# Reordering the first head pair of a clustered-attention and gated-FFN kernel

## The chip, the cores and the metric

The kernel runs on one core of one Trainium2 chip. A core has five engines with a queue of instructions each, run in order: PE (matmuls), DVE (vector), ACT (activations and copies), POOL (a second, slower vector engine) and SP, which here only issues DMA. They wait for each other by semaphores. Matrix results land in PSUM, which the kernel uses as eight banks. The metric is device time in microseconds of one launch, lower is better.

## What is computed

For 4 batches, 8 heads, 768 positions and 64 features, each query and each key is assigned to the nearest of its head's 16 centroids; a query attends only to keys of the same cluster. The result, with the 8 heads side by side (512 features per position), goes through a gated FFN of width 1536.

```python
q_assign = np.argmax(np.einsum('bhsd,hcd->bhsc', q_n, c_n), axis=-1)
k_assign = np.argmax(np.einsum('bhsd,hcd->bhsc', k_n, c_n), axis=-1)
mask = q_assign[:, :, :, None] == k_assign[:, :, None, :]
scores = scale * np.matmul(q, k.transpose(0, 1, 3, 2))
scores = np.where(mask, scores, -1000000000.0)
...
attn = attn / (np.sum(attn, axis=-1, keepdims=True) + 1e-09)
return np.matmul(attn, v).astype(np.float32)
...
x = np.ascontiguousarray(attn_out.transpose(0, 2, 1, 3)).reshape(B * S, H * D)
...
gate = 1.0 / (1.0 + np.exp(-(x @ w_gate)))
val = x @ w_val
return (gate * val @ w_out).astype(np.float32)
```

## The kernel before

**The mask as rows of the matmul.** Each q and k value is split into two fp16 halves (`hl`: high in columns 0 to 63, low in 64 to 127) and turned so that features lie on partitions. Rows 64 to 79 of the turned tile are then overwritten by a one-hot code of the cluster: ones for the key's own cluster, and on the query's side -1920 for every other cluster. One matmul thus gives score plus mask. The cluster comes from 36 small matmuls with the split centroids `cm` (`lg`), a maximum over 16 (`mx`) and a comparison (`oh`). On the query's side the comparison gives 0 or 1, and line 290 multiplies it by -1920.

**Steps.** A step is one `sc` matmul (128 keys by 384 queries, line 451), one exponential on ACT (`es`, line 456) and, two steps later, three `av` matmuls (line 468). Batch 0 runs in two passes of 48 steps, 12 for each of 4 head pairs: pass A (steps 0 to 47) takes the first half of the queries, pass B (48 to 95) the second half with the same keys. The other batches follow with 96 steps each, from step 96 on. From step 60 FFN pieces (`g`, `th`, `v`, `hT`, `o`) are spread over the steps.

**What sets the order.** The program is written out in order; `at(i, f)` puts a piece of preparation behind step i. For pair p of pass A, which starts at step U = 12p, the split (line 549) is at U-23, the three turns at U-16 to U-14, the logits at U-13, the one-hot at U-12 and its placement at U-9. Pair 0 is prepared ahead of step 0, pair 1 mostly so. The turn is six PE transposes into a bank (`t_ps`, line 571) and a copy to SBUF (574 on ACT, 576 on DVE). The placement turns the one-hot (`oh_ps`), copies it to `ohT` (607) and moves its four parts to rows 64 to 79 by four small DMAs from SP, here called hops (line 312): key and query rows of head 0, then of head 1. Only pair 0 is placed without DMA, by copies straight from PSUM (599 to 602), which take turns between DVE and ACT.

**Banks.** All preparation, the scores and the gate and value products of the FFN share one ring of four PSUM banks (line 68); two more (`op`, line 70) are for the FFN's result alone and stand empty until its first result, long after step 66. Two hold `av`.

**Loads.** q, k and v of batch 0 are loaded by SP (and one by ACT) at the start. The six weight DMAs (768 KB each in fp16, cast on the way) are issued from POOL's queue at steps 2, 8, 16 and 22, behind whatever POOL has in front of them.

**Start.** POOL clears `warm` for some dummy matmuls; DVE, ACT and PE make `cm`; DVE splits the keys of head 0 and the queries of pair 0, POOL the keys of head 1; DVE copies `identh`, the fp16 identity that every turn needs (line 640).

## Time and profile before

| | us |
|---|---|
| median of 2 runs | 367.94 (367.67 to 368.2) |
| the profiled execution, by its own clock | 367.52 |
| its span, first to last instruction | 365.7 |

The span lacks 1.8 us of the execution's own time. Stages of the span, each named by its first `sc` or `es`:

| stage | from, us | to, us | length, us |
|---|---|---|---|
| start, up to the first exponential | 0 | 19.61 | 19.61 |
| steps 0 to 11 (pair 0) | 19.61 | 29.39 | 9.78 |
| steps 12 to 23 (pair 1) | 29.39 | 38.53 | 9.14 |
| steps 24 to 35 (pair 2) | 38.53 | 47.26 | 8.73 |
| steps 36 to 47 (pair 3) | 47.26 | 55.83 | 8.57 |
| steps 48 to 71 (half of pass B) | 55.83 | 73.82 | 17.99 |
| the rest | 73.82 | 365.7 | 291.9 |

A row of the timeline gives start, length, engine, line and operation, output from inputs, and in brackets how long the engine was idle before it and what ended that. "PEclk" is the clock that was granted to PE, 1.00 being full speed.

### The profile page before, as it was taken

What the parts mean: (1) busy time and instruction counts of PE and PEld (TensorE: products, weight loads), DVE (VectorE), ACT (ScalarE), POOL (GpSimd) and SP (SyncE); (2) the same over time, 40 slices, a digit from 0 to 9 for tenths busy, and PEclk for the clock granted to TensorE, in tenths of its full rate; (3) what the DMA queues carried; (4) which work ended last, traced back from release to release, by engine and by line L of the source; (5) the groups of instructions that cost most, each with busy time, mean ns of one, the idle gap of its engine ahead of it and who ended that gap; (6) DMA issues with size and microseconds to landing.
All of it is one profiled execution on the core that took longest, in us unless ns stands there. A gap on an engine that the chain in (4) does not pass through costs nothing.

```text
span 365.7 us, 8639 instructions
## 1 busy us (share of the span) xinstructions
PE 332.8 (91%) x3267; PEld 205.7 (56%) x3267; DVE 180.9 (49%) x443; ACT 232.9 (64%) x532; POOL 102.1 (28%) x154
## 2 busy tenths in 40 slices
PE   4688679789998989999999998999999999999995
PEld 1566455456555645546666565556665665565552
DVE  5545434777554837645664555527562442242330
ACT  3276558568677868867887687667877786232321
POOL 6756102521234334340424141323301001000000
PEclk9989969999999989999999999999999999999999
DMA  7839965674769686785665778535752110300102
GB/s 263 258 43 212 203 124 188 144 186 81 214 166 197 178 132 163 152 212 132 178 147 128 132 198 154 145 120 44 102 56 68 59 23 0 109 1 31 58 0 87
DMA packets 82138, 46.53 MB, mean 127 GB/s; under 512 B 61040, under 2 KB 79024, under 8 KB 82096
## 3 DMA queue, kind: packets, MB, share of 16 engines
q1 hardware_dynamic: 78000, 41.03, 47.0%
q0 software_dynamic: 3680, 4.72, 7.6%
q8 instruction: 25, 0.41, 0.4%
q10 hardware_dynamic: 416, 0.23, 0.2%
q14 instruction: 17, 0.14, 0.1%
HBM read 28.34 MB, written 6.29 MB: 95 GB/s over the span
## 4 chain that ended last, share of the span: by engine, by line
PE 70%; DMA 16%; DVE 8%; ACT 3%; issue 2%; POOL 1%; SPq 0%; DVEq 0%; POOLq 0%; ACTq 0%
PE o L358 17%; PE v L341 14%; PE g L326 14%; PE sc L451 12%; DMA T<-hl 10%; PE av L468 7%; DMA TA<-ohT 4%; PE lg L263 2%; ACT es L456 2%; DVE t L225 1%; DVE hT L346 1%; PE t_ps L571 1%; DMA cen<-in_centroids_dram 1%; PE oh_ps L308 1%; DVE vs L184 1%
## 5 line engine op out<-in xcount | busy, mean ns | idle before, releaser
L456 ACT ACTIVATE es<-sc 128x384 f16<-128x384 f32 x384 | 172.7, 492 | 56.1 <-PE sc L451 41.6
L468 PEld LDWEIGHTS <-es 128*128 128x128 f16 x1152 | 81.4, 99 | 49.9 <-ACT es L456 8.2
L468 PE MATMUL av<-va,es 128*128 128x65 f16 x1152 | 99.5, 196 | 2.1 <-ACT es L456 0.9
L346 DVE SCALAR_TENSOR_TENSOR hT<-th,v 128x384 f16<-128x384 f32 x96 | 53.0, 552 | 76.0 <-PE av L468 45.2
L451 PE MATMUL sc<-T 80*128 80x384 f16 x288 | 87.6, 329 | 0.3 <-DVE hT L346 0.2
L358 PE MATMUL o<-wo,hT 128*128 128x512 f16 x288 | 70.3, 378 | 0.0
L332 ACT ACTIVATE th<-g 128x384 f32<-128x384 f32 x96 | 47.1, 491 | 28.0 <-DVE hT L346 16.2
L341 PE MATMUL v<-xTb,wv 128*128 128x384 f16 x288 | 58.6, 325 | 0.3 <-DVE hT L346 0.3
L326 PE MATMUL g<-xTb,wg 128*128 128x384 f16 x288 | 58.5, 325 | 0.0
L227 POOL TENSOR_TENSOR xp<-t,rec 128x384 f16<-128x384 f32 x24 | 20.0, 832 | 113.5 <-issue 66.2
L326 PEld LDWEIGHTS <-wg 128*128 128x128 f16 x384 | 37.5, 98 | 24.1 <-issue 3.5
L341 PEld LDWEIGHTS <-wv 128*128 128x128 f16 x384 | 37.3, 97 | 23.5 <-issue 3.4
L358 PEld LDWEIGHTS <-hT 128*128 128x128 f16 x288 | 27.8, 97 | 26.1
L689 POOL TENSOR_TENSOR hl<-kraw,hl 128x384 f16<-128x384 f32 x24 | 22.1, 922 | 47.2 <-DVE hl L688 27.2
L225 DVE TENSOR_TENSOR t<-av,sv 128x390 f32<-128x390 f32 x32 | 18.0, 561 | 20.6 <-PE av L468 20.3
L451 PEld LDWEIGHTS <-T 80*128 80x128 f16 x288 | 27.8, 97 | 0.6
L689 POOL TENSOR_TENSOR hl<-qraw,hl 128x384 f16<-128x384 f32 x24 | 21.9, 912 | 12.9 <-DVE hl L688 12.6
L367 ACT ACTIVATE ob<-o 128x512 f32<-128x512 f32 x16 | 9.6, 597 | 22.4 <-PE o L358 22.3
L277 DVE TENSOR_TENSOR lgs<-lg,lglo 128x192 f32<-128x192 f32 x24 | 8.5, 355 | 27.7 <-ACT lglo L269 27.5
L451 PE MATMUL sc<-TA 128*128 128x384 f16 x48 | 16.9, 377 | 5.1 <-DMA TA<-ohT 4.9
L184 DVE TENSOR_REDUCE vs<-vraw 128x128 f16<-128x768 f32 x12 | 17.7, 1474 | 0.0
L263 PE MATMUL lg<-cm,T 128*128 128x32 f16 x288 | 11.0, 177 | 6.1 <-DMA T<-hl 6.1
(87 smaller groups left out, 278.0 us busy)
## 6 DMA issues: line engine op xcount, KB each, us to landing
kraw<-in_k_dram SPq DMA_DIRECT2D x16, 384.0 KB, 3.9
vraw<-in_v_dram SPq DMA_DIRECT2D x16, 384.0 KB, 4.8
out_dram<-ob SPq DMA_DIRECT2D x24, 256.0 KB, 2.2
qraw<-in_q_dram SPq DMA_DIRECT2D x12, 384.0 KB, 3.9
wg<-in_moe_w_gate_dram POOLq DMA_DIRECT2D x2, 768.0 KB, 10.3
wv<-in_moe_w_val_dram POOLq DMA_DIRECT2D x2, 768.0 KB, 13.7
wo<-in_moe_w_out_dram POOLq DMA_DIRECT2D x2, 768.0 KB, 15.3
qraw<-in_q_dram SPq DMA_DIRECT2D x7, 192.0 KB, 6.5
```

Source lines behind the costliest of these rows:

```text
L184: DVE.tensor_reduce(s[:, :, 0:64], RAW["v", b, p].rearrange("p h c d -> p h d c"), AX.X, ALU.add)
L225: DVE.tensor_tensor(t, av, sv, ALU.add)
L227: eng.tensor_tensor(x, t[..., 0:64], bcast(r, 64), ALU.mult)
L326: PE.matmul(out=g[:, 0:n], lhsT=wg[fc // WQ][:, dc, fc % WQ, :], rhs=xT[:, dc, t0 : t0 + n], start=(dc == 0), stop=(dc == NDC - 1),)
L332: ACT.activation(th[:, 0:n], g[:, 0:n], AF.Tanh, scale=0.5)
L341: PE.matmul(out=w[:, 0:n], lhsT=wv[fc // WQ][:, dc, fc % WQ, :], rhs=xT[:, dc, t0 : t0 + n], start=(dc == 0), stop=(dc == NDC - 1),)
L346: DVE.scalar_tensor_tensor(hT[:, fc, 0:n], st[0][:, 0:n], 1.0, w[:, 0:n], ALU.add, ALU.mult)
L358: PE.matmul(out=o, lhsT=hT[:, fc, bass.ts(t, 128)], rhs=wo[fc // 6][:, fc % 6, :], start=(fc == 0), stop=(fc == NFC - 1),)
L451: PE.matmul(out=sc.rearrange("p (c t) -> p c t", t=128), lhsT=s["k"], rhs=s["q"], start=True, stop=True,)
L456: ACT.activation(es, sc, AF.Exp, scale=SCALE)
L468: PE.matmul(out=av[:, s["c0"] + i, :], lhsT=s["es"][:, bass.ts(i, 128)], rhs=VA[b, p][:, e, s["j"], :], start=(first and i == 0), stop=(la ...
L689: POOL.tensor_tensor(hl[:, :, 64:128], r, hl[:, :, 0:64], ALU.subtract)
```

## The change

It touches only the start, pass A and the preparation of pass B.

1. **The first pair.** DVE clears `warm` and the one-hot tiles; POOL makes `identh` directly. The first k load becomes two DMAs, one for each head. ACT takes the high halves of both key heads, DVE everything else of pair 0's split. The table load for the exponential moves behind `cm`. `first_place` gives way to `first_pair`, which does logits, one-hot and placement head by head: the turned one-hot of head 0 is placed while DVE marks head 1. `v_cast(0, 0)` goes to ACT.
2. **Banks.** Up to step 66 turns, logits, turned one-hots and sums of v use the two `op` banks (`prep_bank`) and not the ring.
3. **The mask factor** -1920 leaves the one-hot (line 290 is skipped in passes A and B) and is applied in the copies: by a per-partition factor `slot_f` in `a_place`, by a constant in `b_place`, by the scale of the copy in `place`.
4. **Pair 1** is turned and marked in steps 0 to 4 and placed in step 6 by four copies from PSUM (`a_place_direct`), without hops.
5. **Tables.** Pairs 2 and 3: split, turns, logits, one-hot and placement at U-25, U-18, U-14, U-13 and U-11 (two steps earlier, logits and one-hot one); the turn that ACT evicted goes to DVE. Pass B: U-22, U-17, U-14, U-13, U-11 (two to three steps earlier).
6. **Weights.** The first two weight DMAs are issued ahead of step 0, the others at steps 6, 14 and 20.

```diff
+    def prep_bank(n=512, dt=FP, name="bank"):
+
+        if step_no[0] > 66:
+            return bank(n, dt, name)
+        return op.tile([128, n], dt, tag="o", name=name)
...
+    make_identity(nc, identh)
...
+    slot_f = const.tile([128, 1], FP, name="slot_f")
+    DVE.memset(slot_f, 1.0)
+    DVE.memset(slot_f[32:64], MASK)
+    DVE.memset(slot_f[96:128], MASK)
...
-    load(SP, "k", 0, 0)
+    for e in range(2):
+        SP.dma_start(out=RAW["k", 0, 0][:, e], in_=view("k", 0, 0)[:, e])
...
         if first:
-            DVE.tensor_copy(hk[:, 0, :, 0:64], k_[:, 0])
+            for e in range(2):
+                ACT.copy(hk[:, e, :, 0:64], k_[:, e])
+            DVE.tensor_copy(hq[..., 0:64], q_)
             DVE.tensor_tensor(hk[:, 0, :, 64:128], k_[:, 0], hk[:, 0, :, 0:64], ALU.subtract)
-            DVE.tensor_copy(hq[..., 0:64], q_)
             DVE.tensor_tensor(hq[..., 64:128], q_, hq[..., 0:64], ALU.subtract)
-            POOL.tensor_copy(hk[:, 1, :, 0:64], k_[:, 1])
-            POOL.tensor_tensor(hk[:, 1, :, 64:128], k_[:, 1], hk[:, 1, :, 0:64], ALU.subtract)
+            DVE.tensor_tensor(hk[:, 1, :, 64:128], k_[:, 1], hk[:, 1, :, 0:64], ALU.subtract)
...
+    def place(t, ps, slot, c0, n, key, eng):
+        src = ps[32 * slot : 32 * slot + 16, 0 : n * 128].rearrange("p (c t) -> p c t", t=128)
+        dst = t[64:80, c0 : c0 + n, :]
+        if eng is ACT:
+            ACT.activation(dst, src, AF.Copy, scale=1.0 if key else MASK)
+        elif key:
+            DVE.tensor_copy(dst, src)
+        else:
+            DVE.tensor_scalar(dst, src, MASK, None, ALU.mult)
+
+    def a_place_direct(p):
+        ps = oh_turn_pe(st0["oh", p], NCH)
+        t = T["A", p]
+        place(t, ps, 0, 0, 6, True, DVE)
+        place(t, ps, 1, 12, 3, False, ACT)
+        place(t, ps, 2, 6, 6, True, DVE)
+        place(t, ps, 3, 15, 3, False, DVE)
...
-        DVE.tensor_copy(ot.rearrange("p c t -> p (c t)"), ps)
+        DVE.tensor_scalar(ot.rearrange("p c t -> p (c t)"), ps, slot_f, None, ALU.mult)
...
+        mx.append(top(lg[0]))
+        mark(lg[0], mx[0], parts(0), mask=False)
+        mx.append(top(lg[1]))
+        for e in range(2):
+            ps = prep_bank(NCH * 128, HP, name="oh_ps")
+            for c in range(NCH):
+                PE.transpose(ps[0:64, bass.ts(c, 128)], oh[:, c, 64 * e : 64 * e + 64], identh)
+            place(t, ps, 0, 6 * e, 6, True, DVE)
+            place(t, ps, 1, 12 + 3 * e, 3, False, ACT)
+            if e == 0:
+                mark(lg[1], mx[1], parts(1), mask=False)
+                dummies(1)
...
-    A_SPLIT, A_TURN, A_LG, A_PICK, A_PLACE, A_V, A_VS = -23, -16, -13, -12, -9, -7, -3
...
+    load_w(0)
+    dummies(2)
+    first_pair()
+
+    for f, s in (
+        (lambda: a_turn(1, [(0, DVE)]), 0),
+        (lambda: v_sum_pe(0, 0), 0),
+        (lambda: turn_pe(T["A", 1], st0["hl", 1], 6, DVE), 1),
+        (lambda: turn_pe(T["A", 1], st0["hl", 1], 12, DVE), 2),
+        (lambda: a_logits(1), 3),
+        (lambda: a_pick(1), 4),
+        (lambda: a_place_direct(1), 6),
+    ):
+        at(s, f)
+    A_SPLIT, A_TURN, A_LG, A_PICK, A_PLACE, A_V, A_VS = -25, -18, -14, -13, -11, -7, -3
...
-        at(U - 20, lambda p=p: b_split(p))
+        at(U - 22, lambda p=p: b_split(p))
...
```

Three places show how this moves instructions. Lines of the changed kernel have its own numbers.

DVE at the start, before: the splits of pair 0 (`hl`), the identity, the centroids, the copies of the turns (`TA<-t_ps`), the one-hot of both heads and the placement.

```order
L555 CAST hl<-kraw 128x6x64
L556 TENSOR_TENSOR hl<-kraw,hl 128x6x64
L557 CAST hl<-qraw 128x6x64
L558 TENSOR_TENSOR hl<-qraw,hl 128x6x64
L640 CAST identh<-ident 128x128
L169 TENSOR_TENSOR cm<-ct_ps,cm 128x8x16
L576 COPY TA<-t_ps 128x768
L562 CAST hl<-qraw 128x6x64
L281 TENSOR_REDUCE mx<-lg_250 128x18
L283 TENSOR_TENSOR oh_173<-lg_250,mx 128x2x6x16
L283 TENSOR_TENSOR oh_173<-lg_250,mx 128x2x3x16
L290 TENSOR_SCALAR oh_173<-oh_173 128x2x3x16
```

DVE at the start, now.

```order
L575 CAST hl<-qraw 128x6x64
L576 TENSOR_TENSOR hl<-kraw,hl 128x6x64
L577 TENSOR_TENSOR hl<-qraw,hl 128x6x64
L578 TENSOR_TENSOR hl<-kraw,hl 128x6x64
L183 TENSOR_TENSOR cm<-ct_ps,cm 128x8x16
L594 COPY TA<-t_ps 128x768 x2
L580 CAST hl<-qraw 128x6x64
L289 TENSOR_REDUCE mx<-lg_264 128x9
L295 TENSOR_TENSOR oh_139<-lg_264,mx 128x6x16
L295 TENSOR_TENSOR oh_139<-lg_264,mx 128x3x16
L289 TENSOR_REDUCE mx<-lg_283 128x9
L619 COPY TA<-oh_ps 16x768
```

The cast of the keys (L555) and that of the identity (L640) are gone from DVE, a subtraction for head 1 (L578) and a second copy of a turn came to it, and the placement of head 0 (L619) now stands ahead of the one-hot of head 1.

POOL around the first weight DMAs, before: the last split of pair 1's keys is long done, L564 to L566 are pair 2's, and `wg_160` to `wv_163` are weights.

```order
L565 TENSOR_TENSOR hl<-kraw,hl 128x6x64
L564 CAST hl<-kraw 128x6x64
L565 TENSOR_TENSOR hl<-kraw,hl 128x6x64
L566 TENSOR_TENSOR hl<-qraw,hl 128x6x64
L135 DMA wg_160<-in_moe_w_gate_dram 128x4x768
L135 DMA wv_161<-in_moe_w_val_dram 128x4x768
L177 MEMSET va 128x12
L178 CAST va<-vraw 128x12x64
L135 DMA wg_162<-in_moe_w_gate_dram 128x4x768
```

POOL around the first weight DMAs, now: L584 is the last piece of pair 1's split, L582 to L584 behind the DMAs are pair 2's.

```order
L584 TENSOR_TENSOR hl<-qraw,hl 128x6x64
L149 DMA wg_175<-in_moe_w_gate_dram 128x4x768
L149 DMA wv_176<-in_moe_w_val_dram 128x4x768
L582 CAST hl<-kraw 128x6x64
L583 TENSOR_TENSOR hl<-kraw,hl 128x6x64
L582 CAST hl<-kraw 128x6x64
L583 TENSOR_TENSOR hl<-kraw,hl 128x6x64
L584 TENSOR_TENSOR hl<-qraw,hl 128x6x64
L191 MEMSET va 128x12
L192 CAST va<-vraw 128x12x64
L149 DMA wg_177<-in_moe_w_gate_dram 128x4x768
```

The first two weight DMAs moved ahead of pair 2's split; the next two still stand behind it and behind the cast of pair 1's v.

DVE around step 62, before, with the semaphores that each row waits for: splits of batch 1 (L688), the FFN's `hT`, and pair 3's split for pass B (L616).

```order
L688 CAST hl<-kraw 128x6x64 [waits Pool_49]
L688 CAST hl<-kraw 128x6x64 [waits DMAHW4_49,Pool_49]
L688 CAST hl<-qraw 128x6x64
L346 SCALAR_TENSOR_TENSOR hT<-th,v 128x384 [waits PE_49,Activation_49]
L633 COPY ohT<-oh_ps 128x384 [waits DMAHW6_49,DMAHW5_49,PE_49]
L616 CAST hl<-qraw 128x6x64 [waits DMAHW0_49,Pool_49]
L346 SCALAR_TENSOR_TENSOR hT<-th,v 128x384 [waits PE_49,Activation_49]
```

DVE around step 62, now: L668 is pair 3's split for pass B, L744 the splits of batch 1.

```order
L685 TENSOR_SCALAR ohT<-oh_ps 128x384 [waits DMAHW3_49,DMAHW2_49,PE_49]
L668 CAST hl<-qraw 128x6x64 [waits Pool_49]
L744 CAST hl<-kraw 128x6x64 [waits Pool_49]
L744 CAST hl<-kraw 128x6x64 [waits DMAHW1_49,PE_49,Pool_49]
L744 CAST hl<-qraw 128x6x64
L365 SCALAR_TENSOR_TENSOR hT<-th,v 128x384 [waits Activation_49] x2
L594 COPY TB<-t_ps 128x768
```

Pair 3's split moved ahead of batch 1's and lost its wait for a DMA; in its place the second L744 got a wait for PE, and the two `hT` and the copy `TB` behind it have none of their own any more.

More of the change, by code (lines that the diff above doesn't have):

```diff
@@ L177, in v_cast @@
         POOL.memset(va[:, :, :, 64:65], 1.0)
-        POOL.tensor_copy(va[:, :, :, 0:64], RAW["v", b, p])
+        (eng.copy if eng is ACT else eng.tensor_copy)(va[:, :, :, 0:64], RAW["v", b, p])
     def v_sum(b, p):
@@ L281, in pick, with mark @@
         DVE.tensor_reduce(mx[:, 0:n], lg, AX.X, ALU.max)
+        return mx
+    def mark(lg, mx, parts, mask=True):
         for a, z, nh, key, o in parts:
@@ L288, in pick @@
             )
-            if not key:
+            if mask and not key:
                 DVE.tensor_scalar(o, o, MASK, None, ALU.mult)
-    ohs = [const.tile([128, NCH, 128], HP, name=f"oh{i}") for i in range(3)]
+    def pick(lg, parts, mask=True):
+        if isinstance(lg, tuple):
+            ls = smp.tile([128, 12, NCL], FP, name="lgs")
+            n = lg[0].shape[1]
+            DVE.tensor_tensor(ls[:, 0:n], lg[0], lg[1], ALU.add)
+            lg = ls[:, 0:n]
+        mark(lg, top(lg), parts, mask)
     oh_n = [0]
@@ L504 @@
     bg = {}
-    step_no = [0]
     def at(i, f):
@@ L638 @@
     centroid_a()
+    cv = centroid_c()
     a_split(0, True)
[L640 to L643 removed]
+    centroid_d(cv)
+    ACT.activation(r0, warm[:, 0:1], AF.Exp)
     dummies(2)
[L645 to L646 removed]
+    a_turn(0, [(0, ACT), (12, DVE), (6, DVE)])
+    v_cast(0, 0, ACT)
     a_split(1)
[L648 to L656 removed]
+    load_w(0)
[12 more added lines that the diff above has]
+    A_SPLIT, A_TURN, A_LG, A_PICK, A_PLACE, A_V, A_VS = -25, -18, -14, -13, -11, -7, -3
     for p in range(1, NP):
```

102 lines of the change are left out of this document (43 added, 59 removed).

## The prediction

> **What bounds the kernel now.** I read the windows of each stage first, then the chain of waits, then where each stage begins, then the prices of single instructions.
>
> ```profile
> 19.00:29.30 10.30, 8.78 (x149) 6.83 (x146) 4.90 (x14) 6.74 (x14) 6.92 (x11) 0.83 0.49 77
> 29.30:38.50 9.20, 7.13 (x117) 5.30 (x118) 5.54 (x16) 5.83 (x13) 4.01 (x6) 1.00 1.16 212
> 38.50:47.20 8.70, 5.49 (x69) 3.64 (x69) 3.20 (x9) 5.02 (x12) 1.72 (x3) 1.00 1.20 204
> 47.20:55.80 8.60, 7.54 (x77) 5.42 (x78) 3.38 (x10) 5.64 (x12) 0.91 (x1) 0.60 0.56 133
> 55.80:61.10 5.30, 5.02 (x69) 3.10 (x70) 3.11 (x10) 4.30 (x11) 0.91 (x1) 1.00 0.34 109
> 61.10:73.80 12.70, 10.81 (x121) 6.98 (x120) 7.97 (x20) 7.92 (x19) 6.38 (x7) 1.00 0.71 174
> 250.00:310.00 60.00, 59.74 (x578) 37.21 (x575) 26.35 (x61) 45.18 (x105) 10.35 (x17) 1.00 0.28 50
> ```
>
> Columns: length, then busy time of PE, weight load, DVE, ACT and POOL, granted clock, DMA share, GB/s. In pass A (rows 1 to 4) no engine is full, and twelve steps take 8.6 to 10.3 us; the first twelve of pass B, with the same work per step, take 5.3. Late in the span PE is busy 59.74 of 60 us: there nothing of this change can help or be regained, so what the start gains is the total gain.
>
> ```profile
> 9.48 0.86 DVE identh L640
> 10.39 2.10 PE t_ps L571 x18
> ...
> 13.35 0.96 PE lg L254 x36
> ...
> 32.84 5.55 DMA TA<-ohT
> ...
> 41.71 5.42 DMA TA<-ohT
> ```
>
> PE's first turns wait for DVE's splits and for the identity (0.86), and later each pair waits for its own hop (the second of four, head 0's query rows), 5.4 to 5.6 us from issue to landing. The stages begin with these rows, of ACT and PE:
>
> ```profile
> 19.61 0.50 ACT L456 ACTIVATE es<-sc 128x384 f16<-128x384 f32 x1
> 29.39 0.32 PE L451 MATMUL sc<-TA 128*128 128x384 f16 x1 [0.93 <-DMA TA<-ohT]
> 38.53 0.32 PE L451 MATMUL sc<-TA 128*128 128x384 f16 x1 [1.27 <-DMA TA<-ohT]
> 47.26 0.32 PE L451 MATMUL sc<-TA 128*128 128x384 f16 x1 [2.65 <-DMA TA<-ohT]
> ```
>
> Pass B begins where the fourth window ends, at 55.8.
>
> **Term a, the start: first exponential at 15.2 instead of 19.61, -4.4.** Prices of one instruction, and the landing of pair 0's queries:
>
> ```profile
> 5.40 2.43 DVE L555 CAST hl<-kraw 128x384 f16<-128x384 f32 x1
> 6.20 2.30 POOL L646 MEMSET oh<- 128x768 f16 x3
> 7.86 0.56 DVE L556 TENSOR_TENSOR hl<-kraw,hl 128x384 f16<-128x384 f32 x1
> 8.46 0.61 POOL L564 CAST hl<-kraw 128x384 f16<-128x384 f32 x1
> 8.75 0.73 DVE L558 TENSOR_TENSOR hl<-qraw,hl 128x384 f16<-128x384 f32 x1
> L562 DVE CAST hl<-qraw 128x384 f16<-128x384 f32 x2 | 0.7, 352 | 0.0
> L574 ACT COPY TA<-t_ps 128x768 f16<-128x768 f16 x4 | 3.2, 798 | 5.9 <-PE t_ps L571 5.9
> L576 DVE COPY TA<-t_ps 128x768 f16<-128x768 f16 x5 | 2.8, 555 | 4.1 <-PE t_ps L571 4.0
> L283 DVE TENSOR_TENSOR oh<-lg,mx 128x192 f16<-128x192 f32 x3 | 1.1, 358 | 0.2
> L599 DVE COPY TA<-oh_ps 16x768 f16<-16x768 f16 x1 | 0.5, 548 | 0.7 <-PE oh_ps L308 0.7
> L600 ACT COPY TA<-oh_ps 16x384 f16<-16x384 f16 x1 | 0.5, 468 | 4.0 <-DVE TA L599 4.0
> L158 ACT ACT_TABLE_LOAD x1 | 1.3, 1283 | 0.0
> 1.19 0.45 ACTq L106 DMA_DIRECT2D qraw<-in_q_dram  x1
> qraw<-in_q_dram ACTq DMA_DIRECT2D x1, 192.0 KB, 4.4
> ```
>
> The queries land at 1.19+4.4 = 5.6, just as DVE is done with the centroids (L555 follows them at 5.40). DVE then does a cast (0.35) and three subtractions (0.56 to 0.73, taken as 0.65): 7.9. ACT's two casts of the keys have no row; bounded by 0.47 (L600) and 0.80 (L574) each, they lie beside that. ACT has the table load (1.28) between the centroids' copy, near 6.2, and its copy of the first turn (0.80), which so ends near 8.4. With two banks the third turn waits for that copy: six transposes at 2.10/18 are 0.7, DVE's copy 0.55, to 9.6. Logits of both heads (0.96) behind two dummies: 11.1. Head 0's one-hot, bounded by the two L283-like pieces at 0.36 each, runs beside head 1's logits: 11.4. Three dummies hold PE until about 12.1; six transposes 0.6, DVE's copy 0.55, head 1's comparison 0.5, six transposes 0.6, DVE's copy 0.55 and ACT's 0.47 give 15.3. The first exponential is queued behind that last copy on ACT; I take 15.2. With PE's share at full clock it is 14.2, with dummies at half clock and subtractions held 16.6: -5.4 to -3.0. The memsets that moved to DVE (2.30 by POOL's row) and the identity are done before the centroids land and cost nothing; without that cover they would add those 2.3. The cast of v on ACT (0.80) lies in ACT's idle time before the placements, else +0.8. One more load on SP moves the later ones by an issue of 0.45; nothing waits for them then.
>
> L555 took 2.43 us beside POOL's memsets; the same cast takes 0.35 (L562). [...]
>
> **Term b, steps 0 to 11: 10.3 instead of 9.78, +0.5.** Pair 1's preparation now lies in these steps, on DVE: five placements and copies before and at step 6, three more turns, in all some sixteen copies, casts and comparisons at 0.3 to 0.56, 7.7; plus PE parts that DVE waits for with two banks (logits twice, one turned one-hot, one sum, 2.6) and nine hand-overs of about 0.1: 11.2, of which 1.1 lie before the first exponential. Ends: 9.3 without hand-overs, 12.5 with PE at half speed. Step 12 needs no hop any more; its placement by copies, about 2.2, is over before. The mask product leaves DVE; where a copy takes it over I take the copy at its old price, 0.55.
>
> **Term c, steps 12 to 23: 9.3 instead of 9.14, +0.2.** The placement moves two steps up, but on DVE it still stands behind the normalisation of the pair before, which ends at the same place in the steps; so the hop is issued no earlier against step 12. The weights are in flight, hence the hop takes 5.4 again. Step 24 at 15.2+10.3+9.3 = 34.8.
>
> **Term d, steps 24 to 35: 7.3 instead of 8.73, -1.4.** DMA work by stretch, and an undisturbed hop:
>
> ```profile
> 3.00:16.00 13.00, 7.65 (x67) 4.16 (x65) 8.73 (x18) 3.55 (x6) 9.80 (x15) 1.00 1.06 353
> ...
> 24.50:49.50 25.00, 18.64 (x298) 13.63 (x294) 12.09 (x31) 15.65 (x36) 10.36 (x17) 0.98 1.15 199
> 23.07 0.94 POOL L135 DMA_DIRECT2D wg<-in_moe_w_gate_dram  x1
> TB<-ohT SPq DMA_DIRECT2D x8, 12.0 KB, 1.7
> ```
>
> Loads fill the DMA engines until 16, and from 24.5 on the weights fill them for 25.0 us. POOL reaches the first weight DMA near 11, so its data starts 1.4 later, near 12.4, while 3.6 us of loads remain: all weights are in at 12.4+3.6+25.0 = 41 instead of 49.5. Pair 3's hop is issued 3.2 after step 24 (41.71 less 38.53), at 38.0, 3 us before the weights' end. It takes between 1.7 and 5.4; I take 4, two thirds of the way, because the weights are still moving: step 36 at 42.1.
>
> **Term e, steps 36 to 47: 6.5 instead of 8.57, -2.1.**
>
> ```profile
> 17.55:20.97 3.42, 2.25 (x51) 1.73 (x48) 2.27 (x5) 2.13 (x5) 0.00 (x0) 1.00 0.00 0
> 20.97:24.38 3.41, 2.97 (x24) 2.06 (x24) 1.59 (x6) 2.24 (x6) 2.16 (x3) 0.50 0.00 0
> 44.86:48.28 3.42, 1.02 (x23) 0.83 (x24) 0.01 (x1) 0.85 (x3) 0.00 (x0) 1.00 1.25 213
> 48.28:51.69 3.41, 2.63 (x23) 1.79 (x23) 2.68 (x9) 1.82 (x5) 0.00 (x1) 0.50 0.46 77
> ```
>
> After the 2.65 us hole the granted clock is 0.50 from 48.28 on and 0.60 in the stage's mean, and there the one-hot for pass B stood behind the normalisation on DVE; it now comes a step earlier. At full clock the stage would take 5.3 as steps 48 to 59 do, at half clock about 8; the longer hole now is the one at step 24, so most of the half clock falls into steps 24 to 35, where the hop sets the end anyway. I take 6.5, nearer the 5.3 row. [...]
>
> **Term f, steps 48 to 71: -0.8.**
>
> ```profile
> DVE hl L616 <- DMA T<-hl: 2.3, 1, 2.3
> PE t_ps L571 <- POOL hl L617: 0.9, 1, 0.9
> ```
>
> Pair 3's split for pass B waited 2.3 for a transposing DMA, and PE 0.9 for it; that goes. Late next is the split of batch 1 (second L744), which on DVE waits for PE's turn of step 67, with two `hT` behind it; PE has scores and gate products to run meanwhile, so I expect no more than 0.5 from it. Ends: +2 (DVE held for the whole 2.3) and -1.9, the 12.70 less 10.81 us in which PE was idle.
>
> **Sum.** -4.4+0.5+0.2-1.4-2.1-0.8 = -8.0. From the profiled execution's 367.52 that is 359.5; the median of the two runs lies 0.42 above it, so 359.9, told as 360.0.
>
> **Rivals.** (1) The hops keep the lead: the third hop costs 5.4 as well, and PE stays at half clock after it. Then d is 0 (3.2+5.4 is the old 8.7 again), e is -0.6, the sum -5.1 and the time 362.8. For it speaks that all three hops cost nearly the same. [...] (3) The hops cost under 3 us, as those of pass B do, and no stage waits for one: steps 12 to 23 and 24 to 35 then take about 7.0 each (9.14 and 8.73 with holes of 1.27 and 2.65 taken off, and a little for the freed ring), c is -2.1 and d -1.7, in sum 357.3; against it all three hops beside the weights. (4) Slower: with two banks, preparation and steps wait for each other in all three first pairs. A pair has about ten turns, sums and logits for which PE must have a bank back from DVE; at 30 of them it decides from 8.0/30 = 0.27 us each over what I counted, and at 0.4 the time is 372. No quoted row shows a hold of that size, but the ring had four banks.
>
> **Chances.** My forecast (358 to 361.5) 0.50, rival 1 0.24, rival 2 0.08, rival 3 0.14, rival 4 0.04. Two per cent, about what a measurement of this kernel can tell from no change, is 7.36 us, so the line is at 360.6. Faster: 0.35 of the forecast's 0.50, rival 3 and a sliver, 0.50; slower 0.02; the same 0.48. The range runs from 356 (rival 3 with 1.3 us less) to 364.5 (rival 1 with 1.7 us more).
>
> **What would show it.** First exponential near 15.2; no hop before step 12; hops of step 24 near 5.4 and of step 36 shorter; weights landed near 41; first score of pass B near 48.6, step 72's near 66. Wrong if DVE's casts at the start again take over 2 us, if PE waits over 1 us for a bank in steps 0 to 11, or if PE waits at step 68 for `hT`.

## The result and the profile after

| | before | after |
|---|---|---|
| median, us | 367.94 (2 runs) | 354.05 (353.22 to 354.87, 2 runs) |
| ratio | | 0.962, 95% interval 0.952 to 0.972 |
| profiled execution: its own time, span | 367.52, 365.7 | 353.22, 351.4 |

The changed kernel is faster by 13.9 us, where 8 were predicted, and 354.05 lies under the predicted range of 356 to 364.5. Run again six times it gave a median of 355.98 (352.62 to 358.11), ratio 0.962 (0.957 to 0.967). All eight executions have a mean of 355.4; two of them, 358.04 and 358.11, count as slow, because they lie over 1.5% above the fastest, and the other six have a mean of 354.4.

The windows of the stages after, with the columns of before (length, busy time of PE, weight load, DVE, ACT and POOL, granted clock, DMA share, GB/s); the first four are steps 0 to 47 in twelves, the fifth steps 48 to 71:

```profile
13.80:24.00 10.20, 7.91 (x162) 6.69 (x162) 6.77 (x16) 5.66 (x13) 7.52 (x12) 1.00 1.15 236
24.00:32.50 8.50, 6.65 (x121) 5.21 (x119) 6.24 (x16) 5.80 (x13) 3.34 (x5) 1.00 1.18 211
32.50:40.20 7.70, 6.41 (x82) 4.76 (x82) 3.83 (x10) 5.36 (x12) 1.72 (x3) 0.78 0.99 170
40.20:46.70 6.50, 5.57 (x78) 3.52 (x79) 3.19 (x9) 5.02 (x12) 0.91 (x1) 1.00 0.22 63
46.70:63.00 16.30, 15.12 (x186) 10.04 (x186) 10.06 (x27) 12.33 (x29) 7.26 (x8) 1.00 0.58 172
```

The rows of the timeline with which stages begin (first exponential, first scores of steps 24 and 36); step 12 now waits for no DMA:

```profile
13.83 0.49 ACT L475 ACTIVATE es<-sc 128x384 f16<-128x384 f32 x1
...
32.52 0.32 PE L470 MATMUL sc<-TA 128*128 128x384 f16 x1 [1.49 <-DMA TA<-ohT]
...
40.19 0.32 PE L470 MATMUL sc<-TA 128*128 128x384 f16 x1 [1.27 <-DMA TA<-ohT]
```

| stage | before, us | after, us | difference | predicted |
|---|---|---|---|---|
| start (a) | 19.61 | 13.83 | -5.8 | -4.4 |
| steps 0 to 11 (b) | 9.78 | 10.15 | +0.4 | +0.5 |
| 12 to 23 (c) | 9.14 | 8.54 | -0.6 | +0.2 |
| 24 to 35 (d) | 8.73 | 7.67 | -1.1 | -1.4 |
| 36 to 47 (e) | 8.57 | 6.52 | -2.1 | -2.1 |
| 48 to 71 (f) | 17.99 | 16.29 | -1.7 | -0.8 |
| the rest | 291.9 | 288.4 | -3.5 | 0 |

The prediction's sum falls short in four places: the start, steps 12 to 23, pass B and, most of all, the rest. Of the rest's 3.5 us, 2.9 lie in batch 1 (steps 96 to 191), where the change moves no instruction. The windows of that batch, before and after:

```profile
96.12:158.13 62.01, 54.51 (x610) 34.29 (x609) 36.34 (x94) 48.36 (x118) 23.93 (x35) 0.97 0.78 179
```

```profile
84.50:143.64 59.14, 52.98 (x610) 33.55 (x609) 36.38 (x95) 47.77 (x118) 23.93 (x35) 1.00 0.76 192
```

PE runs the same 610 matmuls in 62.01 and in 59.14 us. Before, it stood idle for 7.5 us there (62.01 less 54.51), and its clock was not full: one window with PE busy 1.73 of 3.41 is followed by one at half clock, here called a half-clock spell. Of the 2.9 us, 1.5 are busy time (54.51 against 52.98) and 1.3 idle time (7.5 against 6.2).

```profile
130.19:133.60 3.41, 1.73 (x27) 1.14 (x25) 0.55 (x1) 1.79 (x5) 0.90 (x2) 1.00 1.15 155
133.60:137.01 3.41, 3.41 (x33) 2.06 (x30) 1.33 (x5) 2.27 (x5) 0.00 (x0) 0.50 0.51 99
```

The list of waits names the largest part of the idle time: PE's logits wait for the transposing DMA that turns the split halves (`T<-hl`). The two rows, before and then after, are of the whole span (us in total, times, longest); in batch 1 alone the waits sum to 4.8 and 3.3.

```profile
PE lg L263 <- DMA T<-hl: 6.1, 7, 1.7
```

```profile
PE lg L277 <- DMA T<-hl: 4.5, 4, 1.4
```

### The profile page after: what moved, and what is told of

It is laid out like the page before. It is cut to its first block, busy times and chain, and to the rows that moved or that the text cites. A ratio compares the mean times of both kernels' runs of the same rounds, so it can differ in the third digit from the quotient of the medians.

```text
span 351.4 us, 8653 instructions
## 1 busy us (share of the span) xinstructions
PE 326.8 (93%) x3274; PEld 202.2 (58%) x3274; DVE 181.0 (51%) x449; ACT 231.3 (66%) x532; POOL 97.8 (28%) x149
## 4 chain that ended last, share of the span: by engine, by line
PE 72%; DMA 5%; DVE 3%; ACT 3%; issue 2%; POOL 1%; SPq 0%; ACTq 0%; DVEq 0%
PE o L377 18%; PE v L360 16%; PE g L345 15%; PE sc L470 12%; PE av L487 7%; DMA T<-hl 5%; ACT es L475 3%; PE lg L277 2%; DVE hT L365 1%; DVE vs L198 1%; DVE hl L744 1%; DVE t L239 0%; POOL hl L745 0%; PE vs_ps L204 0%; DVE oh L295 0%
## 5 line engine op out<-in xcount | busy, mean ns | idle before, releaser
L487 PEld LDWEIGHTS <-es 128*128 128x128 f16 x1152 | 80.2, 98 | 48.9 <-ACT es L475 8.3
L487 PE MATMUL av<-va,es 128*128 128x65 f16 x1152 | 97.9, 194 | 2.7 <-ACT es L475 1.1
L470 PE MATMUL sc<-T 80*128 80x384 f16 x288 | 86.7, 327 | 0.3 <-DVE hT L365 0.2
L470 PE MATMUL sc<-TA 128*128 128x384 f16 x48 | 15.6, 348 | 2.8 <-DMA TA<-ohT 2.8
L384 DVE TENSOR_SCALAR ob<-o 128x512 f32<-128x512 f32 x8 | 5.5, 690 | 21.0 <-PE o L377 21.0
```

Of the source, the lines that this page charges most:

```text
L470: PE.matmul(out=sc.rearrange("p (c t) -> p c t", t=128), lhsT=s["k"], rhs=s["q"], start=True, stop=True,)
L487: PE.matmul(out=av[:, s["c0"] + i, :], lhsT=s["es"][:, bass.ts(i, 128)], rhs=VA[b, p][:, e, s["j"], :], start=(first and i == 0), stop=(la ...
```

## The experiments

Stage lengths below are taken between the first DVE instruction of the normalisations (`t<-av`), which stand two steps behind each head pair's last score. They are steadier than the time: behind step 36 the two traces of the changed kernel agree within 0.1 us up to batch 1.

| us | first exponential | 0-11 | 12-23 | 24-35 | 36-47 | 48-59 | 60-71 | 72-83 |
|---|---|---|---|---|---|---|---|---|
| before | 19.61 | 10.48 | 9.14 | 9.04 | 7.76 | 7.99 | 12.95 | 9.85 |
| after | 13.83 | 11.28 | 8.11 | 7.68 | 6.01 | 7.50 | 11.99 | 8.79 |
| after, again | 14.53 | 10.72 | 8.35 | 7.23 | 6.01 | 7.50 | 11.98 | 8.80 |
| old start | 18.94 | 10.74 | 9.67 | 6.31 | 6.01 | 7.50 | 11.99 | 8.79 |
| old weight issue | 14.43 | 10.66 | 8.96 | 8.05 | 6.01 | 7.50 | 11.98 | 8.80 |
| ring of four | 13.88 | 9.79 | 8.40 | 7.82 | 6.01 | 7.45 | 12.22 | 8.79 |
| old table, pass B | 15.01 | 12.22 | 11.15 | 7.11 | 6.07 | 7.63 | 12.50 | 9.84 |
| old table, pairs 2, 3 | 15.78 | 11.48 | 8.12 | 7.80 | 6.01 | 7.49 | 11.99 | 8.80 |
| pair 1 by hops | 14.51 | 11.14 | 7.94 | 7.81 | 6.01 | 7.50 | 11.99 | 8.79 |
| old mask factor | 14.72 | 11.09 | 8.90 | 6.26 | 6.01 | 7.50 | 11.99 | 8.79 |

**The changed kernel once more.**

> The changed kernel once more, unaltered, as the base of the runs that undo a part. Theory 'stages' (the gain is 5.8 us of start, 3.3 us of steps 12 to 47 and the rest in stages behind step 48, all set by the order of the program): 354.0 within 0.5, first exponential near 13.8, the same two waits for hops at steps 24 and 36. Theory 'clock' (a good part of the gain is half-clock spells of 3.4 us that were escaped by chance of where the 3.4 us windows lie: four in the trace before, one in the trace after): the number of half-clock spells in the new trace is not one, and each spell more costs up to 1.7 us, so 354.0 to 356.

Six executions spread over 5.5 us. The trace of the fastest, 352.62, is like the first: waits of 1.73 and 0.81 for hops, one half-clock spell at the same place. The spread does not follow the clock alone (358.04 at a mean clock of 0.994, 358.11 at 0.976), so neither theory holds it all; the first fits the traces.

**Undoing the start.**

> The changed kernel with the start of before: one k load, clears of the dummies' input and of the one-hot tiles on POOL, identity copied on DVE, the old split, turns with two copies on ACT, logits, one-hot and placement of both heads together, v cast on POOL. Pair 1 is still turned in steps 0 to 2. Theory 'start adds in full': first exponential near 18.8 (19.61 less the 0.8 of pair 1's turn that stood ahead of it), so 5.0 later and 359.0. Theory 'start is absorbed by the hops': the weights land at the same 38.7, so the hops of pairs 2 and 3, now issued later, meet fewer bytes; 2 us or more of the 5.0 come back by step 48 and the time is 357 or less. With a further half-clock spell at step 0 up to 1.7 more.

```diff
+    DVE.tensor_copy(identh, ident)
...
+    a_turn(0, [(0, ACT), (12, DVE), (6, ACT)])
...
-    v_cast(0, 0, ACT)
...
-    first_pair()
+    a_logits(0)
...
+    a_pick(0)
+    v_cast(0, 0)
+    first_place()
...
```

359.37 us, ratio 0.975 (0.971 to 0.979); first exponential at 18.94. By step 48 the kernel is 4.8 us behind: the start adds in full. It also shows what a hop costs once the weights are in. The landing times of pair 2's four hops, and of pair 3's, issued from 41.3 on (the DMA share is 1.26 in the microsecond from 40 and 0.17 in that from 42):

```profile
L327 SPq DMA_DIRECT2D TA<-ohT x4: 567/707/807, 31.7 to 34.2; - x4
...
DMA to landing us min/median/max: 5.5/5.9/6.7
...
L327 SPq DMA_DIRECT2D TA<-ohT x4: 507/540/580, 41.3 to 43.2; - x4
...
DMA to landing us min/median/max: 1.7/1.8/2.0
```

Same shapes, same sizes: 5.9 us beside the weights, 1.8 behind them, and no wait at step 36.

**Undoing the weight issue.**

> The changed kernel with the weight DMAs issued at steps 2, 8, 16 and 22 again. Theory 'weights set the hops' (the term d of the prediction): first weights move from 10.8 to about 16, the last land near 43 instead of 38.7; the hop of pair 3 then costs its 5.4 and the wait at step 36 grows from 1.27 to about 3: 355.5 to 357. Theory 'hops cost the same' (the queue's own latency and not the weights): waits at steps 24 and 36 stay within 0.3 of 1.49 and 1.27 and the time is 354.0.

```diff
-    load_w(0)
...
+    at(2, lambda: load_w(0))
+    at(8, lambda: load_w(1))
+    at(16, lambda: load_wo(0))
+    at(22, lambda: load_wo(1))
```

356.10, ratio 0.965 (0.961 to 0.969). The weights end some 4 us later (the DMA share falls under 1 in the microsecond from 42 instead of from 38), the waits for hops are 2.10 and 1.56, and the kernel is 1.2 us behind by step 48. The direction is the first theory's, but the wait at step 36, which by it grows to about 3, grew to 1.56 only; the time alone does not tell.

**Undoing the banks.**

> The changed kernel with all preparation in the ring of four banks again, the two result banks empty up to the FFN's first result. Theory 'banks free the steps': scores wait for a ring bank behind preparation that DVE holds, in steps 0 to 11 and in steps 48 to 83, where PE's idle time went from 3.2 to 1.9 us; the time rises by 1 to 2.5, to 355 to 356.5. Theory 'banks do nothing': 354.0 within 0.5. Theory 'two banks hold back' (the fourth rival): PE no longer waits 0.79, 1.05 and 1.62 for copies by DVE and ACT in the start and in steps 0 to 11, and the time falls to 352 or 353.

```diff
     def prep_bank(n=512, dt=FP, name="bank"):
-        if step_no[0] > 66:
-            return bank(n, dt, name)
-        return op.tile([128, n], dt, tag="o", name=name)
+        return bank(n, dt, name)
```

354.42, ratio 0.959 (0.955 to 0.963). Steps 0 to 11 are shorter by 0.9 to 1.5 and pass B is as long as with the two banks (60 to 71 0.2 longer). The two banks give next to nothing and hold the steps beside pair 1 back: the third theory, as far as the trace goes.

**Undoing the table of pass B.**

> The changed kernel with the old table for pass B (split, turn, logits, one-hot and placement two to three steps later). Read by stage lengths between the normalisations of head pairs, which agree within 0.1 us between the two traces of the changed kernel behind step 36 (steps 36 to 47 6.01, 48 to 59 7.50, 60 to 71 11.99, 72 to 83 8.79). Theory 'the table of pass B': the lengths go back towards the 7.99, 12.95 and 9.85 of before, 2.0 to 2.5 us in sum, and steps 36 to 47 gain 0.5 to 1; the mean of the runs (355.4 in eight runs of the changed kernel) rises to 358. Theory 'batch 1 comes in earlier' (loads, splits and the FFN meet the steps otherwise because the start is shorter, whatever the table): the lengths stay within 0.3.

```diff
-        at(U - 22, lambda p=p: b_split(p))
+        at(U - 20, lambda p=p: b_split(p))
...
```

357.75, ratio 0.978 (0.969 to 0.986). Steps 48 to 83 take 1.7 us more, 1.05 of it in steps 72 to 83, where the old length of before is back to 0.01. Steps 36 to 47 do not change. PE's list of waits shows both what the table does and what it doesn't:

```profile
PE sc L470 <- DMA TA<-ohT: 4.1, 1, 4.1
...
PE t_ps L589 <- POOL hl L669: 1.4, 1, 1.4
```

The second row is the table: PE waits for pair 3's split on POOL, as it did before (0.9). The first, a 4.1 us wait at step 24, is not: the program up to step 25 is the same as in the changed kernel, but two half-clock spells fell into the start and steps 0 to 11 of this execution, and its hops took up to 7.2. So the profiled execution's 359.21 overstates the table; the 1.7 us of steps 48 to 83 are its measure.

**Undoing the table of pairs 2 and 3; pair 1 by hops; the mask factor.**

> The changed kernel with the old table for pairs 2 and 3 of pass A (two steps later, logits and one-hot one) and the second turn on ACT. The prediction's step c says that the hop is issued no earlier against its step, because the copy stands behind the normalisation on DVE: by it the waits at steps 24 and 36 stay near 1.5 and 1.0 and the time does not change. Theory 'two steps earlier are two steps less to wait': each hop is issued about 1.2 us later against its step, both waits grow by that, steps 12 to 35 take 2 to 2.5 us more, and more half-clock spells follow the longer holes.

```diff
-    A_SPLIT, A_TURN, A_LG, A_PICK, A_PLACE, A_V, A_VS = -25, -18, -14, -13, -11, -7, -3
+    A_SPLIT, A_TURN, A_LG, A_PICK, A_PLACE, A_V, A_VS = -23, -16, -13, -12, -9, -7, -3
...
```

355.72, ratio 0.973 (0.964 to 0.982). Steps 12 to 35 take 15.92 us, against 15.79 and 15.58: the table does nothing, as step c had it. The hop is issued 2.2 us behind the normalisation here (29.46 less 27.26) and 2.1 behind it in the changed kernel (27.16 less 25.11).

> The changed kernel with pair 1 placed by hops (at step 6, turned and marked in steps 0 to 4 as now). Theory 'the hop of pair 1 sets step 12': issued about 1.3 us behind the one-hot at 17.9, near 19.5, and 4.7 to 5.4 on the way, its second part lands near 25, step 12 waits about 1 for it instead of 0 at 23.98; three copies of 0.56 leave DVE, so steps 0 to 11 take 0.5 to 1.5 us more. Theory 'the copies cost as much as the hop' (DVE is the bound of steps 0 to 11): no change within 0.3, since 1.6 us of copies go.

```diff
...
-        (lambda: a_place_direct(1), 6),
+        (lambda: a_place(1), 6),
...
```

354.15, ratio 0.969 (0.960 to 0.979). Step 12 waits 2.21 for the hop, and steps 0 to 11 are as long as in the changed kernel (11.14 against 11.28 and 10.72): the copies cost about what the hop cost. The edit also puts the sum of v (`v_sum_pe`) ahead of pair 1's first turn.

> The changed kernel with the factor -1920 applied to the one-hot on DVE again (0.56 for head pairs of pass A, 0.20 for pass B) and plain copies. Theory 'it stands in the chain': first exponential 0.2 to 0.5 later, hops of pairs 2 and 3 later by 0.3 to 0.5 each, 1 us in all. Theory 'the factor in the copy costs the copy what it saves': no stage changes by more than 0.3.

```diff
-        DVE.tensor_scalar(ot.rearrange("p c t -> p (c t)"), ps, slot_f, None, ALU.mult)
+        DVE.tensor_copy(ot.rearrange("p c t -> p (c t)"), ps)
...
```

358.55 (353.31 to 358.90), ratio 0.972 (0.955 to 0.989), too wide to tell; in the trace step 48 is reached within 0.1 us of the changed kernel (46.98 against 46.91 and 46.84), so no cost shows.

**Where batch 1 gains: a wait, or the place of the buffers.** First the logits of batches 1 to 3 two steps later, in both kernels.

> The kernel before with the logits and the one-hot of batches 1 to 3 two steps later (and their turned one-hot and hops with them); nothing else. It tests the 2.9 us that the change gained in batch 1 (steps 96 to 191: 62.0 us before, 59.1 after), where it moved no instruction. Theory 'one wait, one spell': before, PE's five waits for transposing DMAs (4.8 us) make one 3.4 us window with PE busy only 1.73, and the next runs at half clock; without the waits the spell near 133 goes too, steps 96 to 191 take 57 to 58.5 and the time falls by 3.5 to 5, to 363 to 364. Theory 'the waits hide other waits' (PE would wait for the exponentials or DVE then): steps 96 to 191 stay above 60.5 and the time within 1.5 of 367.5.

```diff
-            at(s + gap + 9, lambda e=e: lgt(e))
+            at(s + gap + 11, lambda e=e: lgt(e))
...
```

366.29, ratio 0.998 (0.994 to 1.002): nothing. (Its trace is that of the longest of ten executions, 370.12, and is not read by stages.)

> The changed kernel with the same shift of batches 1 to 3. Theory 'one wait, one spell': PE's waits for transposing DMAs there are 3.3 us in the first trace of the changed kernel and 2.7 in the second, without a spell; most of them go, steps 96 to 191 take 57 to 58 instead of 59.1, and the mean of the runs falls from 355.4 to 353.5. Theory 'the waits hide other waits': within 0.5 of 59.1.

353.84, ratio 0.962 (0.957 to 0.967): PE's wait for `T<-hl` in batch 1 falls from 3.3 to 2.3, but its wait for DVE's sums of v grows from 0.9 to 3.0, and batch 1 takes 60.1 instead of 59.1. Here the waits hid other waits, as the second theory has it.

What the change did to those DMAs is in no line that moves an instruction. Its new tile `slot_f` has 4 bytes per partition and takes 32, so the buffers behind it start 32 bytes further on (first tile of each, bytes in a partition, in the built program):

```
              hl               T
before        98528 (32 mod 64, 224 mod 256)    112352 (32 mod 64, 224 mod 256)
after         98560 ( 0 mod 64,   0 mod 256)    112384 ( 0 mod 64,   0 mod 256)
```

> The kernel before with one more tile of 4 bytes per partition (it takes 32) behind the matrix of ones, and nothing else. In the changed kernel the new tile for the mask's factors moves every later SBUF buffer by 32 bytes: the split halves and their turned tiles start at 32 modulo 64 before and at 0 after. The fastest transposing DMA from the one to the other took 3.7 us in both traces of the old layout and 3.2 in all eleven of the new one. Theory 'layout': 3.2 here too, the one of the attention's output slower in turn (2.6 before, 3.2 to 3.5 after), PE's waits for the transposing DMAs in batch 1 fall from 4.8 to about 3, steps 96 to 191 from 62.0 to 59 to 60.5, and the time by 1.5 to 3, to 365 to 366.5. Theory 'neighbours' (the 0.5 comes from what else is in flight or from the order of the queues): 3.7 and 367.5.

```diff
     POOL.memset(ones, 1.0)
+    pad = const.tile([128, 1], FP, name="pad")
+    POOL.memset(pad, 0.0)
```

365.07, ratio 0.988 (0.984 to 0.993), 3.7 us under before in the same session (368.76). Batch 1 takes 57.95, without a half-clock spell, and PE's waits for `T<-hl` in it sum to 1.9. Of the output's two transposing DMAs the small one, whose median the expectation gave, was not slowed (`xB<-xp`, at the fastest 2.3, before 2.4); the larger one was (`xTb<-xp`, 2.7, before 2.5; rows below).

> The changed kernel with the same tile added, which moves the buffers to 32 modulo 64 again. Theory 'layout': fastest transposing DMA of the split halves 3.7, PE's waits for them in batch 1 from 3 to 4.5, steps 96 to 191 60.5 to 62 instead of 59.1, with a half-clock spell in some runs; mean of the runs 357 to 358 instead of 355.4. Theory 'neighbours': 3.2 and the stages unchanged within 0.3.

The same two lines in the changed kernel: 358.82, ratio 0.973 (0.970 to 0.976), 3.4 above the mean of 355.4 and 4.4 above that of 354.4; batch 1 takes 64.45, with two half-clock spells. Now one side of the DMA at a time.

> The changed kernel with the seven turned tiles T alone moved to 32 modulo 64 (32 bytes ahead of them and 32 behind, so that all other buffers keep their place modulo 64). Theory 'target': the fastest transposing DMA of the split halves takes 3.7 here and PE's waits in batch 1 grow to 4 or more; the mean of the runs 357 to 359. Theory 'source': 3.2 and 355.4.

> The changed kernel with the three split tiles hl alone moved to 32 modulo 64, all others kept. Theory 'target': 3.2 and 355.4. Theory 'source': 3.7, and the mean of the runs 357 to 359. If both kernels show 3.7, either side is enough; if both show 3.2 the two must coincide.

```diff
+    pad1 = pool("pad1", 1)
     hlp = pool("hl", 3)
+    pad2 = pool("pad2", 1)
     tp = pool("T", 7)
...
```

(For the target the pads stand around `tp`.) 354.28, ratio 0.963 (0.957 to 0.968), with the target moved; 357.97, ratio 0.975 (0.966 to 0.983), with the source moved. Batch 1 takes 61.22 and 62.67, each time with one half-clock spell, and PE's waits for `T<-hl` in it sum to 3.7 and 5.3. What answers for the split halves in each trace (issues, landing time): before, changed, before with a pad, changed with a pad, target moved, source moved.

```profile
L247 SPq DMA_TRANSPOSE T<-hl x24: 1425/1460/3326, 66.8 to 263.7; - x24
...
DMA to landing us min/median/max: 3.7/3.7/6.9
```

```profile
L261 SPq DMA_TRANSPOSE T<-hl x24: 1301/1422/3422, 58.5 to 248.7; - x24
...
DMA to landing us min/median/max: 3.2/3.3/7.7
```

```profile
L249 SPq DMA_TRANSPOSE T<-hl x24: 1393/1432/3586, 65.1 to 257.7; - x24
...
DMA to landing us min/median/max: 3.2/3.2/7.1
```

```profile
L263 SPq DMA_TRANSPOSE T<-hl x24: 1301/1447/3405, 58.9 to 254.6; - x24
...
DMA to landing us min/median/max: 3.7/3.8/7.5
```

```profile
L265 SPq DMA_TRANSPOSE T<-hl x24: 1301/1423/3514, 58.1 to 250.5; - x24
...
DMA to landing us min/median/max: 3.2/3.3/7.2
```

```profile
L265 SPq DMA_TRANSPOSE T<-hl x24: 1302/1450/3274, 59.1 to 252.5; - x24
...
DMA to landing us min/median/max: 3.7/3.8/7.0
```

Read the minimum and median: 3.2 to 3.3 where the source starts at 0 modulo 64, 3.7 to 3.8 where it starts at 32, whatever the target. The source sets it. For this DMA all starts tried at 0 modulo 64 are also at 0 modulo 256.

Two other transposing DMAs, both of 128x768, tell 64 and 256 apart, because the pads moved their sources along (starts in the built programs): that of the output from batch 1 on (`xTb<-xp`) and that of the one-hot (`ohT<-oh`). First the output's, before (source at 0 modulo 256) and in the kernel `x4_align` below (source at 64):

```profile
L479 SPq DMA_TRANSPOSE xTb<-xp x12: 1211/1228/1590, 115.1 to 310.8; - x12
...
DMA to landing us min/median/max: 2.5/2.8/4.0
```

```profile
L498 SPq DMA_TRANSPOSE xTb<-xp x12: 1210/1240/2205, 101.4 to 293.0; - x12
...
DMA to landing us min/median/max: 2.7/2.9/4.1
```

Then the one-hot's, before with a pad (source at 0 modulo 256, target at 224) and changed with a pad (source at 192, target at 0):

```profile
L704 SPq DMA_TRANSPOSE ohT<-oh x12: 1212/1227/2189, 80.2 to 266.5; - x12
...
DMA to landing us min/median/max: 2.5/3.4/5.5
```

```profile
L760 SPq DMA_TRANSPOSE ohT<-oh x12: 1212/1230/2597, 71.9 to 263.0; - x12
...
DMA to landing us min/median/max: 2.7/2.8/5.6
```

Here the fastest landing is read, since the median also holds waits behind other transfers. In all nineteen traces it is 2.5 where the source starts at 0 modulo 256 (`xTb<-xp` in two traces, `ohT<-oh` in one) and 2.7 elsewhere. Starts at 64 and 192, multiples of 64 too, landed later. Of the starts run (0, 32, 64, 96, 160, 192 and 224 modulo 256) 0 alone landed sooner; 128 was in no run.

Side and size are thus measured: 3.7 for sources at 224 (before) and at 32 modulo 256 (source moved), 3.2 at 0; 2.7 for sources at 64 and 192, 2.5 at 0. Why a start elsewhere lands later is not shown.

**A faster version.**

> The changed kernel with all preparation in the ring of four banks and pairs 2 and 3 placed by four copies as pair 1 is, eight steps ahead, so that pass A has no hop at all. It leaves the weights as they are. Theory 'the hop behind the weights sets steps 24 and 36' (hops took 3.4 to 7.2 us while weights were in flight and 1.7 to 2.0 behind them): both waits and the half-clock spell at 33 go; steps 12 to 23 fall from 8.1 to 6.7, steps 24 to 35 from 7.7 to 6.3; with 1.0 from the ring in steps 0 to 11 the time is 350 to 351.5. Theory 'DVE is the bound of pass A anyway' (pair 1 cost the same by hops and by copies): the copies, 2.2 us a pair less 0.56, take the place of the waits; 353.5 to 354.5.

```diff
-            at(U + A_PLACE, lambda p=p: a_place(p))
+            at(U - 8, lambda p=p: a_place_direct(p))
...
```

350.47, ratio 0.953 (0.947 to 0.960): the first theory. Pass A has no hop and its trace no half-clock spell before 118.

> Both of the two edits above in one kernel. If they add, the time is 1.5 us under that of the direct placement alone: 348.5 to 350 by the first theories of each, 352 to 353.5 by the second ones.

348.86 (348.66 to 349.59), ratio 0.949 (0.943 to 0.955), the fastest and steadiest: the trace has full clock from end to end. Its windows of steps 0 to 47:

```profile
13.10:22.90 9.80, 8.70 (x165) 6.87 (x164) 7.14 (x19) 6.49 (x15) 8.10 (x12) 1.00 1.15 253
22.90:30.70 7.80, 6.76 (x118) 5.18 (x117) 6.01 (x15) 5.59 (x14) 3.35 (x5) 1.00 1.16 209
30.70:37.40 6.70, 5.61 (x86) 3.95 (x84) 4.81 (x14) 5.64 (x15) 1.72 (x3) 1.00 1.24 208
37.40:43.40 6.00, 4.93 (x72) 3.13 (x70) 3.19 (x9) 4.64 (x12) 0.91 (x1) 1.00 0.49 116
```

The weights still fill the DMA engines (share 1.16 and 1.24), but nothing in steps 12 to 35 waits for a small DMA behind them.

> The fastest kernel so far (ring of four banks, direct placement of pairs 2 and 3, logits of batches 1 to 3 two steps later; 348.9) with a tile of 32 bytes ahead of the attention's output, so that the tiles of both transposing DMAs start at 0 modulo 64. Theory 'layout': the transposing DMA of the output falls from 3.2 to 2.6 in the first pass and the split halves stay at 3.2; its waits are few, so the time falls by 0 to 1, to 348 to 349. Theory 'neighbours': no change of either.

349.71, ratio 0.948 (0.944 to 0.951): no further gain. The tile put the output's source at 64 modulo 256 and not at 0, where by the rows above nothing is won: `xTb<-xp` stays at 2.7 at the fastest, and `xB<-xp` has a median of 2.9 instead of 2.8. What fails is the expectation's 64; the output's source at 0 was not run in this kernel.

## Why the prediction was right and wrong

**The rest: wrong, and the largest miss.** The sentence "there nothing of this change can help or be regained, so what the start gains is the total gain" failed twice. It was read from a window at 250 to 310; between step 72 and the end of batch 1 PE was not full (7.5 us idle in batch 1 alone). And it took the change for a change of order only. Shown: the 32 bytes of `slot_f` are worth 3.7 us in the kernel before and 3.4 to 4.4 in the changed one, through the source of the transposing DMA (moved alone 357.97, against 354.28 with the target moved). With a second pad, that is with the change but without this effect, the kernel takes 358.82, inside the forecast's 358 to 361.5.

How 0.5 us per DMA becomes that is shown in part. In the three traces read by stages with the source off a multiple of 256 (before, changed with a pad, source moved), PE's waits for `T<-hl` in batch 1 sum to 4.8 to 5.8 and the batch takes 62.0 to 64.5; in the fifteen with the source on one the waits are 1.7 to 4.0 and the batch takes 58.0 to 61.2. All three have one or two half-clock spells in that batch, of the fifteen only four have one. That the longer waits bring the spells on is argued and not shown.

**Term f: right mechanism, too small.** Predicted -0.8 in steps 48 to 71. The table of pass B is worth 1.7 by the undoing, 1.05 of it in steps 72 to 83, which the term left out. Of the shortening of steps 48 to 71 that leaves 0.8 (7.99 and 12.95 to 7.63 and 12.50) which no undone part brings back; its cause stays open. Pair 3's split is on time, and the turn of batch 1 behind it cost nothing: PE has no wait over 0.25 us for `hT` near step 68.

**Term a: right mechanism, 1.4 us too small.** Part of the first trace's surplus is chance: the centroids landed 0.65 earlier than before (first used at 3.06 instead of 3.71), and ACT's copy of the first turn, which stands behind them and the table load, ends at 7.95 instead of the sum's 8.4. In the second trace of the same kernel they were used at 3.52 and the first exponential came at 14.53; over the fifteen traces with this order of the start it came between 13.10 and 15.78. A further 0.6 is a dummy pair that the sum put on the path. It runs beside DVE's last copy, and the logits, of which only head 1's need that copy, start before it ends (rows of the timeline after). Some 0.3 is left unassigned.

```profile
3.06 0.23 DVE L169 TENSOR_TENSOR sq<-cen 128x64 f32<-128x64 f32 x1 [0.37 <-DMA cen<-in_centroids_dram]
...
7.17 0.78 ACT L592 COPY TA<-t_ps 128x768 f16<-128x768 f16 x1
...
8.33 0.59 PE L562 MATMUL wm<-warm 128*128 128x512 f16 x2
...
8.54 0.56 DVE L594 COPY TA<-t_ps 128x768 f16<-128x768 f16 x1 [0.99 <-PE t_ps L589]
...
8.77 1.05 PE L268 MATMUL lg<-cm,TA 128*128 128x16 f16 x36
```

The slow end of this term's range (16.6) has subtractions that are held. No run shows such a hold. Before, DVE's L558 took 0.73 beside a POOL cast (8.46 to 9.07), 0.17 more than L556. In the changed kernel all three subtractions took 0.55, but it was hardly put to the test there: POOL's first cast began at 6.34, when only the third of them (6.30 to 6.85) was still running. That cast took 0.88 where the next took 0.51, so here POOL was the slower one, not DVE:

```profile
6.30 0.55 DVE L578 TENSOR_TENSOR hl<-kraw,hl 128x384 f16<-128x384 f32 x1
```

```profile
6.34 0.88 POOL L582 CAST hl<-kraw 128x384 f16<-128x384 f32 x1 [4.29 <-DMA kraw<-in_k_dram]
```

**Term b: right in size.** 10.15 against 10.3 (the text's own numbers, 11.2 less 1.1, give 10.1). Of the waits for a bank that the text gave as a sign of trouble one was there, 1.62 behind pair 1's placement; another of 1.05 lay in the start, where the sum had it. The fourth rival, two banks holding the steps, is real, but costs 1 us and only beside pair 1.

**Term c: one half right.** The hop is issued no earlier against its step; the undone table shows it. But it took 4.6 to 4.9 us beside the weights and not 5.4, so the stage is 8.54 and not 9.3.

**Term d: right.** The weights end near 38.7 (41 was taken), pair 3's hop takes 3.4 to 4.5 (4 was taken). The half-clock spell fell into steps 24 to 35 (clock 0.78), as said. Neither the first rival (this hop too at 5.4) nor the third (all hops under 3) came about.

**Term e: right number, by luck.** Steps 36 to 47 take 6.52 against 6.5. But the 6.5 was a mix of 5.3 at full clock and 8 at half clock, and the stage ran at full clock (1.00) all through: 5.3 was too little. That the one-hot of pass B comes a step earlier has no part in it, as the undone table shows. And most of the gain was the clock's: before with a pad, with the old pass A, the stage had full clock too and took 7.05 (8.57 in the trace before), because there the spells fell elsewhere:

```profile
47.10:54.15 7.05, 5.47 (x79) 3.57 (x80) 3.38 (x10) 5.02 (x12) 0.91 (x1) 1.00 0.46 79
```

Two windows of the changed kernel show the spell and what came ahead of it:

```profile
29.81:33.22 3.41, 1.92 (x55) 1.70 (x52) 1.12 (x4) 1.26 (x3) 0.00 (x0) 1.00 1.24 217
33.22:36.63 3.41, 3.41 (x30) 2.23 (x28) 2.47 (x6) 2.46 (x7) 1.09 (x3) 0.50 1.23 203
```

In the first one PE was busy for 1.92 of 3.41 us, more than half, and the clock of the next was 0.50. Before, too, a window with PE busy 2.25 of 3.42 (17.55 to 20.97) stood ahead of one at 0.50.

**What no single part brings back.** The changed kernel is 9.1 us ahead by step 48 (46.91 against 56.03 at the normalisation). Undone one at a time, the start brings back 4.8 of this and the weights 1.2, while the banks take 1.0 off; the mask factor and pair 1's copies bring back 0.5 at most. (The traces of the two tables, with half-clock spells in the start, tell nothing here.) So some 4 us come back with no single part. Where the half-clock spells fall is in this: the old pass A reaches the same point at 56.03 before and at 54.34 before with a pad. How much the parts do together stays open.

## What to carry to other kernels

Before a stretch is called closed to a change, read its own windows: idle time of PE there is open to anything that moves a DMA by half a microsecond (3.7 to 3.2 here), and a new small tile moves every buffer behind it (here by 32 bytes), so compare the start addresses of what the DMAs read as well as the order. A small DMA that someone waits for should not stand behind bulk loads (pair 2's hops took 5.9 us beside the weights here, pair 3's 1.8 behind them, with the old start); replacing the last eight hops of pass A by copies was worth some 4 us here (354.42 with the ring alone, 350.47 with both). Undo the parts of a change one at a time and read stage lengths beside times: of the six parts here the start (4.8) and the table of pass B (1.7) carried most, the weights 1.2, the mask factor and pair 1 nothing, and the banks cost about 1.
